# Issuing the input loads of batch 4 one phase earlier in a fused attention and feed-forward kernel

## Chip, cores and metric

The kernel runs on one core of a Trainium2 chip (trn2). The metric is the device time of one execution in microseconds (us). A profile's own span is some 1.7 to 1.9 us shorter than the device time of the same run.

## The reference

Eight batches of eight heads, 576 positions of 64 numbers. For each head, q is exponentiated and normalised along its 64 numbers, k along its 576 positions; the attention is linear. The result feeds a two-layer network with an exact GELU:

```python
q_s = softmax(q, axis=-1); k_s = softmax(k, axis=2)
kv  = einsum('bhsd,bhse->bhde', k_s, v)
x   = einsum('bhsd,bhde->bhse', q_s, kv)      # to (4608, 512), heads side by side
h   = x @ w_in                                 # 512 -> 2048
out = (0.5 * h * (1 + erf(h / sqrt(2)))) @ w_out   # 2048 -> 512, float32
```

## The kernel before

The tokens are worked in nine chunks: chunk c is 512 of the 576 positions of batch c, chunk 8 is what is left over of all batches. A chunk has a w_in phase (64 matmuls and 16 GELUs) and an output phase (four output tiles of 16 matmuls). In chunk c's phases the attention of later batches is prepared: loads, exponentials (ScalarE), normalisation (VectorE, GpSimd), a transpose by DMA, casts of v (VectorE), small matmuls. The parts that matter:

```python
def load(b):                       # three DMAs: 1024, 1152 and 1152 KB, two buffers each
    load_main(b, "q", q)
    load_pair(b, "k", k)
    load_pair(b, "v", v)

def cast_v_all(b):                 # four VectorE casts of v to bf16
    for hp in range(HP):
        cast_v(b, hp)

def y_out(c, ps, j):               # empties an output tile and stores it
    y_sb = moe_sb.tile([128, DM], FP32, tag="y_sb")     # four buffers
    nc.vector.tensor_copy(out=y_sb, in_=ps)
    ...
        nc.sync.dma_start(out=dst, in_=y_sb)

def y_phase(c, ins):
    for j in range(J - 1 if c == B else J):
        ps = psum_y.tile([128, DM], FP32, tag="y")      # two buffers
        for t in range(NDF):
            y_mm(c, ps, j, t)
            for f in ins.get((j, t), []):               # work hung in after matmul t of tile j
                f()
        y_out(c, ps, j)
...
y_phase(1, {
    (0, 15): [lambda: norm_q(2, 0, 2)],
    (1, 1): [lambda: norm_q(2, 1, 2, nc.vector)],
    (1, 12): [lambda: kv_step(2)],
    (1, 15): [lambda: xbar_step(2)],                    # the transpose by DMA
    (2, 2): [lambda: cast_v_all(3)],
    (3, 5): [lambda: x_all(2), lambda: kv_step(3)],
})

def front3():                      # hung into the w_in phase of chunk 2
    norm_q(3, 0, 2)
    norm_q(3, 1, 2, nc.vector)
    xbar_step(3)
    load(4)
...
    # chunk 2 onwards, nb = c + 2: hung into the output phase
    yi[(1, 0)] = [lambda nb=nb: norm_q(nb)]
    if nb < B:
        yi[(0, 8)] = [lambda nb=nb: cast_v_all(nb)]
    yi[(3, 0)] = [lambda nb=nb: xbar_step(nb)]
```

All loads, stores and transposes are issued by one queue (SyncE), in program order; only half of the last stores go by ScalarE's.

The softmax here doesn't subtract the row's maximum and nothing guards it: scores larger than these inputs give would overflow.

## Time and profile before

| | before |
|---|---|
| time, median of the first three runs | 283.32 us (283.0 to 283.43) |
| span of the profiled run | 281.7 us |
| TensorE busy | 272.7 us, 97% |
| VectorE, ScalarE, GpSimd busy | 36%, 56%, 12% |
| granted TensorE clock | 1.000 |

The page gives busy times, forty slices of the span, and a chain of waits that is followed back from the last instruction. TensorE is the bound from about 15 us on (busy 261.14 of the 263.20 us from there to 278.20). These lines of the chain show where TensorE's work ends (start, length, what); the span goes on to 281.66.

```profile
274.40 3.51 PE ps L326 x32
...
277.93 0.29 DVE y_sb L331
```

### The profile page before, as it was taken

To read this page: it belongs to the slowest core of one execution; us is meant where nothing else is said; L and a number is where in the kernel's file an instruction comes from. 1 tells how busy PE (TensorE), PEld (TensorE's weight loads), DVE (VectorE), ACT (ScalarE), POOL (GpSimd) and SP (SyncE) were. 2 spreads that over 40 slices of the span, in tenths; PEclk is the share of its full clock that TensorE was granted. 3 is DMA by queue.
4 is the path that set the end of the run, shared out by engine and by line. 5 is a ranking of instruction groups with operands and counts; after the bars stand their busy time and mean duration, and the time that the engine had idled before them with its cause. 6 is when DMAs were issued, how large, how long until landed. Compare 5 with 4: busy or idle time off the path is not lost.

```text
span 281.7 us, 4584 instructions
## 1 busy us (share of the span) xinstructions
PE 272.7 (97%) x1937; PEld 126.0 (45%) x1937; DVE 101.8 (36%) x149; ACT 156.8 (56%) x242; POOL 32.9 (12%) x25
## 2 busy tenths in 40 slices
PE   8789999999999899999999999999999999999994
PEld 3334454444444344444444444444444444444443
DVE  2766586309750570075006510562006200230021
ACT  5766754689467815693469436852683264036400
POOL 1530040002020050005000500050005000000000
PEclk9999999999999999999999999999999999999999
DMA  7999999952439329901990179226501500210033
GB/s 236 381 404 428 398 404 404 403 227 60 132 94 353 151 95 249 367 37 40 229 388 37 58 193 349 92 77 169 132 0 74 149 2 0 77 74 0 2 74 75
DMA packets 44851, 50.09 MB, mean 178 GB/s; under 512 B 20384, under 2 KB 29856, under 8 KB 44576
## 3 DMA queue, kind: packets, MB, share of 16 engines
q1 hardware_dynamic: 44544, 49.68, 51.7%
q8 instruction: 15, 0.25, 0.3%
q10 hardware_dynamic: 288, 0.13, 0.2%
q14 instruction: 4, 0.03, 0.0%
HBM read 36.70 MB, written 9.44 MB: 164 GB/s over the span
## 4 chain that ended last, share of the span: by engine, by line
PE 73%; DMA 18%; DVE 4%; ACT 2%; SPq 1%; issue 1%; ACTq 0%
PE ps L294 34%; PE ps L304 34%; DMA f<-in_v_dram 9%; DMA f<-in_q_dram 4%; DMA w<-in_moe_w_in_dram 3%; DMA touch<-in_moe_w_in_dram 2%; PE kv L165 2%; PE ps L250 1%; PE ps L326 1%; DVE v_aug L144 1%; DVE qsum L195 1%; ACT ek L137 1%; ACT e L132 1%; DVE e L197 1%; SPq L230 0%
## 5 line engine op out<-in xcount | busy, mean ns | idle before, releaser
L294 PE MATMUL ps<-xT,wi_bf 128*128 128x512 bf16 x576 | 126.1, 379 | 0.2 <-DVE wi_bf L378 0.2
L304 PE MATMUL ps<-wo_bf,g 128*128 128x512 bf16 x560 | 124.4, 379 | 1.3 <-DVE y_sb L311 1.3
L299 ACT ACTIVATE g<-ps 128x512 bf16<-128x512 f32 x144 | 85.6, 597 | 67.6 <-PE ps L294 67.6
L294 PEld LDWEIGHTS <-wi_bf 128*128 128x128 bf16 x576 | 56.1, 98 | 68.6 <-DVE wi_bf L378 0.7
L304 PEld LDWEIGHTS <-g 128*128 128x128 bf16 x560 | 53.9, 98 | 65.7 <-issue 1.9
L311 DVE COPY y_sb<-ps 128x512 f32<-128x512 f32 x35 | 23.9, 684 | 75.9 <-PE ps L304 75.6
L197 POOL TENSOR_TENSOR e<-e,recq 128x2048 bf16<-128x2048 bf16 (+1 forms) x9 | 25.7, 2857 | 178.0 <-DVE recq L196 145.9
L144 DVE CAST v_aug<-f 128x576 bf16<-128x576 f32 x26 | 17.9, 746 | 57.2 <-DMA f<-in_v_dram 57.2
L276 ACT CAST xT<-ps 128x512 bf16<-128x512 f32 x19 | 10.2, 588 | 31.0 <-PE ps L250 21.4
L195 DVE TENSOR_REDUCE qsum<-e 128x16 f32<-128x1024 bf16 (+1 forms) x13 | 21.0, 1614 | 15.1 <-ACT e L132 15.1
L132 ACT ACTIVATE e<-f 128x512 bf16<-128x512 f32 (+1 forms) x42 | 20.5, 556 | 1.8 <-DMA f<-in_q_dram 1.5
L137 ACT ACTIVATE ek<-f 128x2304 bf16<-128x2304 f32 (+1 forms) x10 | 17.2, 1730 | 3.1 <-DMA f<-in_k_dram 3.1
L274 DVE CAST xT<-ps 128x512 bf16<-128x512 f32 x15 | 9.7, 686 | 15.3 <-PE ps L250 12.4
L78 ACT ACT_TABLE_LOAD x9 | 11.5, 1283 | 2.8 <-issue 2.6
L404 PE MATMUL ps<-zeros 128*128 128x512 bf16 x29 | 8.8, 462 | 1.2 <-DVE scr L73 1.2
L132 ACT ACT_TABLE_LOAD x7 | 9.0, 1283 | 0.1
L165 PEld LDWEIGHTS <-ek 64*64 64x64 bf16 x576 | 6.6, 105 | 3.4 <-issue 1.2
L165 PE MATMUL kv<-v_aug,ek 64*64 64x65 bf16 x576 | 7.1, 193 | 0.7 <-POOL v_aug L144 0.4
L378 DVE CAST wi_bf<-w 128x512 bf16<-128x512 f32 (+1 forms) x8 | 7.1, 907 | 1.8 <-DMA w<-in_moe_w_in_dram 1.7
L397 DVE CAST wo_bf<-w 128x2048 bf16<-128x2048 f32 (+1 forms) x5 | 5.1, 1014 | 4.7 <-DMA w<-in_moe_w_out_dram 4.7
L197 DVE TENSOR_TENSOR e<-e,recq 128x1024 bf16<-128x1024 bf16 x4 | 6.4, 1606 | 0.1
L250 PE MATMUL ps<-qT,kvc 64*64 64x512 bf16 x60 | 5.0, 390 | 1.1 <-DVE kvc L176 1.0
(31 smaller groups left out, 41.1 us busy)
## 6 DMA issues: line engine op xcount, KB each, us to landing
out_dram<-y_sb SPq DMA_DIRECT2D x32, 256.0 KB, 2.3
f<-in_k_dram SPq DMA_DIRECT2D x6, 1152.0 KB, 9.5
f<-in_v_dram SPq DMA_DIRECT2D x6, 1152.0 KB, 11.4
f<-in_q_dram SPq DMA_DIRECT2D x6, 1024.0 KB, 7.1
w<-in_moe_w_in_dram SPq DMA_DIRECT2D x6, 512.0 KB, 7.9
f<-in_k_dram SPq DMA_DIRECT2D x4, 576.0 KB, 10.7
f<-in_v_dram SPq DMA_DIRECT2D x8, 288.0 KB, 8.4
f<-in_q_dram SPq DMA_DIRECT2D x4, 512.0 KB, 8.6
```

The source lines that it names most:

```text
L78: nc.scalar.activation(out=scr[:, 1:2], in_=scr[:, 0:1], func=func)
L132: nc.scalar.activation(out=dst[:, i], in_=src[:, u], func=AF.Exp)
L137: nc.scalar.activation(out=ek[b % 2][:, i:i + n], in_=st[b]["kf"][:, i:i + n].rearrange("p x (n d) -> p x n d", n=NS), func=AF.Exp,)
L144: eng.tensor_copy(out=v_aug[b % 2][:, hp, :, 0:D], in_=st[b]["vf"][:, hp, :].rearrange("p (n d) -> p n d", n=NS),)
L165: nc.tensor.matmul(ps[c, i, half, 0:D + 1], ek[b % 2][pr, hp, n, :], v_aug[b % 2][pr, hp, n, 0:D + 1], start=(n == 0), stop=(n == NS - 1),)
L195: nc.vector.reduce_sum(out=qsum, in_=eq[:, :, hs, :], axis=AX.X)
L197: eng.tensor_tensor(out=eq[:, :, hs, :], in0=eq[:, :, hs, :], in1=recq.unsqueeze(3).to_broadcast([128, J, w, D]), op=ALU.mult,)
L276: nc.scalar.copy(out=st[b]["xT"][:, hp, :], in_=ps)
L294: nc.tensor.matmul(ps, wi_bf[:, dm, t * 128:(t + 1) * 128], xT[:, dm, :], start=(dm == 0), stop=(dm == NDM - 1),)
L299: nc.scalar.activation(out=g[:, t, :], in_=ps, func=AF.Gelu)
L304: nc.tensor.matmul(ps, st[c]["g"][:, t, j * 128:(j + 1) * 128], wo_bf[:, t, :], start=(t == 0), stop=(t == NDF - 1),)
L311: nc.vector.tensor_copy(out=y_sb, in_=ps)
```

## The change

The loads of batch 4 waited in the issue queue behind the transpose of batch 3. The intent is to issue them one phase earlier, when their buffers have long been free.

```diff
-        (2, 2): [lambda: cast_v_all(3)],
+        (2, 2): [lambda: cast_v_all(3), lambda: load(4)],
...
         xbar_step(3)
-        load(4)
```

## The prediction

> **What bounds the kernel now.** I read the page first (busy shares, slices, chain), then the waits of TensorE, then a table by stage, then the timelines of VectorE and of the DMA-issuing queue around the one place where the chain leaves TensorE.
>
> ```profile
> PE 272.7 (97%) x1937; PEld 126.0 (45%) x1937; DVE 101.8 (36%) x149; ACT 156.8 (56%) x242; POOL 32.9 (12%) x25
> PEclk9999999999999999999999999999999999999999
> DMA  7999999952439329901990179226501500210033
> ```
>
> TensorE is busy 97% of the span at the full granted clock; all the others have room, and DMA is full only at the start and then in bursts, one per batch. TensorE sets the end. So the question is only whether the change moves an idle time of TensorE. In the whole stretch from 60 us to the end, the list of waits of TensorE has one row:
>
> ```profile
> PE ps L304 <- DVE y_sb L311: 1.3, 1, 1.3
> ```
>
> Line 304 is the output matmul, line 311 the copy that empties its PSUM tile. The wait happens once. The stage table puts it in a chunk. Its six rows are the hidden-layer (w_in) phase and the output phase of chunks 2, 3 and 4 in turn (start and end, length, then busy time by engine, clock, DMA share, GB/s):
>
> ```profile
> 76.26:90.07 13.81, 13.81 (x65) 6.27 (x64) 5.15 (x6) 8.79 (x15) 1.90 (x1) 1.00 0.60 185
> 90.07:106.60 16.53, 15.27 (x146) 7.13 (x144) 8.82 (x13) 8.64 (x11) 3.62 (x1) 1.00 0.39 149
> 106.60:120.41 13.81, 13.81 (x65) 6.27 (x64) 0.95 (x2) 8.96 (x15) 0.00 (x0) 1.00 0.95 304
> 120.41:135.54 15.13, 15.13 (x146) 7.16 (x145) 8.88 (x13) 8.64 (x11) 3.62 (x1) 1.00 0.19 61
> 135.54:149.35 13.81, 13.81 (x66) 6.26 (x65) 0.72 (x2) 8.96 (x15) 0.00 (x0) 1.00 0.90 296
> 149.35:164.47 15.12, 15.12 (x146) 7.12 (x145) 9.11 (x13) 8.64 (x11) 3.62 (x1) 1.00 0.19 60
> ```
>
> The w_in phases all take 13.81 us. The output phase of chunk 2 takes 16.53 where those of chunks 3 and 4, with the same work, take 15.13 and 15.12. The excess of 1.40 us is the only irregularity left. Its cause is in the chain of waits:
>
> ```profile
> 83.24 0.63 SPq L89
> ...
> 83.91 0.71 SPq L97
> ...
> 84.67 10.32 DMA f<-in_v_dram
> ...
> 95.01 2.73 DVE v_aug L144 x4
> 97.75 0.61 DVE y_sb L311
> ...
> 98.40 2.97 PE ps L304 x13
> ```
>
> The three issues at 83.24 to 85.18 us are q, k and v of batch 4, the very loads that the change moves. The v load lands at 94.99. The four casts of v (2.73 us) stand in VectorE's order ahead of the copy that empties the first output tile, so that copy starts at 97.66 and the third output tile, which reuses the same one of two PSUM tiles, starts at 98.40 where TensorE was ready at 97.14. The timeline of VectorE shows that nothing but the load held it:
>
> ```profile
> 79.96 1.75 DVE L197 TENSOR_TENSOR e<-e,recq 128x1024 bf16<-128x1024 bf16 x1
> 95.01 2.73 DVE L144 CAST v_aug<-f 128x576 bf16<-128x576 f32 x4 [13.30 <-DMA f<-in_v_dram]
> 97.66 0.68 DVE L311 COPY y_sb<-ps 128x512 f32<-128x512 f32 x1
> ```
>
> 13.30 us idle before the casts, ended by the v load.
>
> [...] batch 4 is issued 13.9 us before its phase boundary needs it (83.24 against 97.14) and takes 11.75 us to 94.99, and the casts and copy do not fit in the rest. [...] loads already follow the transpose of batch 3 by 0.05 us. [...] Here the rotation is two deep, so a copy that is late by more than one output tile (16 matmuls, about 3.5 us) stalls TensorE; the 1.26 us stall is that.
>
> **The change part by part.** Nothing is added or removed: the same three DMAs (1024, 1152 and 1152 KB), the same buffers, one core. Only the place in program order moves.
>
> Old place: behind the transpose of batch 3 in the issue queue, which waits for VectorE's normalisation to end at 81.71. Hence 83.24.
>
> New place: in the output phase of chunk 1, after its third output tile's third matmul. In the issue queue that is behind the transpose of batch 2 and the second store of chunk 1:
>
> ```profile
> 68.39 1.97 SPq L230 DMA_TRANSPOSE qT<-e  x1
> 70.46 7.05 SPq L314 DMA_DIRECT2D out_dram<-y_sb  x3
> 81.86 1.33 SPq L230 DMA_TRANSPOSE qT<-e  x1
> ```
>
> The second store takes 0.34 us to issue, so q is issued at about 70.46 + 0.34 + 0.05 = 70.85. Are the input buffers free? They are those of batch 2: its exponentials end on ScalarE at about 66.6, and its v was cast in chunk 1's w_in phase. Yes, so there is no new wait at the issue. The three issues take 0.63 + 0.71 + 0.51 and gaps, about 1.95 us, to 72.8, which is when the next store becomes ready (its copy ends at 72.77). So the issue queue loses nothing.
>
> Landing: with the old 11.75 us from the issue of q to the landing of v, v lands at about 70.85 + 11.75 = 82.6. VectorE is free from 81.71. The casts run at 82.6 to 85.3, inside the 13.30 us that VectorE sat idle. Then the first output tile of chunk 2 (ends about 90.07 + 3.5 = 93.6) is copied by 94.4, ahead of the 97.14 at which TensorE wants the PSUM tile: 2.7 us to spare, as in chunk 3, where the copy starts 3.66 us after the phase (124.07 against 120.41).
>
> The sum: chunk 2's output phase goes from 16.53 to about 15.13. That is the stall of 1.26 us plus 0.14 us that the table shows as longer busy time of the same matmuls (15.27 against 15.13), which I take for the restart after the stall. Everything after 98.40 is an unbroken TensorE chain to the last tile, so the saving passes whole to the end: 283.32 - 1.40 = 281.9 us. The next load, of batch 5, is issued after chunk 2's last store and so moves with TensorE; in chunk 3 its casts (120.15) already come before the first output copy (124.07).
>
> What earns nothing: q and k of batch 4 come earlier too, but the exponentials at 92.18 and 94.28 follow one another on ScalarE without a wait for them. Normalising batch 4 and its transpose start some 3 us earlier, and TensorE never waited for them.
>
> **The rivals.**
>
> (a) A collision with the transpose of batch 2. It is issued at 68.39, lands about 4.1 us later, at 72.5, and TensorE uses it at 72.89: only 0.4 us of slack, on the bounding engine. The loads now start right behind it. Against harm: they are behind it and behind a store in the same queue[...]; batch 3's transpose, with loads right behind it, landed in 3.7 us. If loads still shared the DMA engines with it, a landing 1 us late would cost 0.6 us, and the time would be about 282.5.
>
> (b) The wait moves to another place. The two stores of chunk 1 and the transpose of batch 3 now stand behind 3.3 MB of loads. The stores may land after 11 us; there are four output buffers, and the first to be reused is needed after 93. The transpose of batch 3 is issued at 81.86 with the loads nearly drained, and its product is used near 100. Even if the issue queue were held up by a full backlog (at start-up one k issue took 4.80 us), there are many us of room. This would leave the time at 281.9; only if it delayed the transpose by over 12 us would the gain go.
>
> (c) The load is hidden anyway and nothing changes, 283.3. The listed wait and the 16.53 against 15.13 speak against this.
>
> (d) DMA traffic slows the engines. The w_in phases at DMA shares of 0.60, 0.95 and 0.90 all take 13.81, so no.
>
> **Range and chances.** 281.9 us, a gain of 0.5%. The three runs of before lie within 0.43 us, and rival (a) can cost some tenths; a small shift in the loads at the start could move either side a little. Range 281.3 to 282.6. Since even removing all idle time left after 60 us is worth 0.5%, over 2% (5.7 us) in either direction needs a mechanism that I don't see: 1% faster, 98% same, 1% slower.
>
> **What would show each step.** Right: the list of TensorE's waits loses its row of 1.3 us from the output copy; batch 4's loads are issued near 71 and its casts begin near 82.6; the output phase of chunk 2 takes about 15.1 us; every later event is 1.3 to 1.4 us earlier. Wrong: a TensorE gap before the attention matmuls at 72.9 or a transpose of batch 2 landing in over 4.5 us (rival a); casts beginning later than 94 (the loads held by something I missed); or an output phase of chunk 1 that has grown.

The 11 us of rival (b) is the longest landing of a store in the profile before (11.0; median 2.3).

## The result, and the profile after

| | before | after |
|---|---|---|
| median, 6 runs each | 283.26 us (282.64 to 283.58) | 282.6 us (281.98 to 283.68) |
| ratio | | 0.998, 95% interval 0.9959 to 1.0001 |
| span of the profiled run | 281.66 us | 280.79 us |

A ratio is the mean time of one kernel's fast runs over that of the other's fast runs of the same rounds, so not quite the ratio of the medians. 0.998 is 0.57 us. The forecast was 1.40. By this first timing even the 0.57 is not clear of zero: the interval reaches 1.0001.

Yet the stage that the prediction was about became as short as it said. The stage table of the changed kernel, its rows of the output phases of chunks 2 and 3:

```profile
89.93:105.05 15.12, 15.12 (x145) 7.11 (x144) 6.41 (x9) 8.64 (x11) 3.62 (x1) 1.00 0.19 61
...
118.86:133.98 15.12, 15.12 (x146) 7.14 (x145) 9.02 (x13) 8.64 (x11) 3.62 (x1) 1.00 0.19 61
```

The output phase of chunk 2 takes 15.12 us, like that of chunk 3; it had taken 16.53. The list of TensorE's waits has no row left from 44 us to the end. The timelines of the issue queue and of VectorE show the steps: q is issued at 70.89, the casts begin at 85.28 (before: 95.01), and the output copy waits for TensorE at 93.59, not the other way about.

```profile
70.89 0.42 SPq L89 DMA_DIRECT2D f<-in_q_dram  x1
71.41 0.66 SPq L97 DMA_DIRECT2D f<-in_k_dram  x1
72.11 0.51 SPq L97 DMA_DIRECT2D f<-in_v_dram  x1
```

```profile
85.28 2.73 DVE L144 CAST v_aug<-f 128x576 bf16<-128x576 f32 x4 [3.71 <-DMA f<-in_v_dram]
93.59 0.69 DVE L311 COPY y_sb<-ps 128x512 f32<-128x512 f32 x1 [5.58 <-PE ps L304]
```

The end of the chain, after:

```profile
272.86 3.51 PE ps L326 x32
...
276.38 0.29 DVE y_sb L331
```

TensorE and the last copy finish 1.55 us earlier than before (276.38 against 277.93), but the span only 0.87 us earlier. What follows the last copy has grown. The DMA view of that last stretch shows it, before (from 278.3 us on) and then after (from 276.7 us on): queues with packets, MB and share, and the last two stores with KB and us from issue to landing.

```profile
q1 hardware_dynamic: 160, 0.13, 16.7%
q10 hardware_dynamic: 160, 0.13, 12.8%
...
out_dram<-y_sb SPq DMA_DIRECT2D x1, 32.0 KB, 2.0
out_dram<-y_sb ACTq DMA_DIRECT2D x1, 32.0 KB, 2.1
```

```profile
q1 hardware_dynamic: 160, 0.13, 13.9%
q10 hardware_dynamic: 160, 0.13, 11.2%
q14 instruction: 1, 0.01, 0.5%
...
out_dram<-y_sb SPq DMA_DIRECT2D x1, 32.0 KB, 3.0
out_dram<-y_sb ACTq DMA_DIRECT2D x1, 32.0 KB, 3.1
```

After, one instruction fetch (8 KB, on queue 14) runs while the last stores are under way, and they land 3.0 and 3.1 us after their issue, not 2.0 and 2.1. Before, that fetch comes when all is over. The only difference in VectorE's instruction list is one wait for a semaphore, in front of the first output copy of chunk 2 (193 instructions before, 194 after); SyncE too has one wait more (171 instructions before, 172 after). I read the wait as follows: before, the cast's wait for the v load covered what the copy needed, and now that it waits on another semaphore, the copy needs one of its own. The semaphore records agree: before, the v load and the cast's wait used semaphore 109; after, both use 105, and the added wait is for 109. No run tested it apart from that.

### The profile page after: what moved, and what is told of

The parts are those of the page before. It is cut to its first block, busy times and chain, and to the rows that moved or that the text cites. A ratio compares the mean times of both kernels' runs of the same rounds, so it can differ in the third digit from the quotient of the medians.

```text
span 280.8 us, 4586 instructions
## 1 busy us (share of the span) xinstructions
PE 273.0 (97%) x1937; PEld 125.9 (45%) x1937; DVE 102.1 (36%) x149; ACT 156.8 (56%) x242; POOL 32.9 (12%) x25
## 4 chain that ended last, share of the span: by engine, by line
PE 89%; DMA 6%; ACT 2%; SPq 1%; DVE 1%; issue 1%; ACTq 0%
PE ps L294 43%; PE ps L304 41%; DMA w<-in_moe_w_in_dram 3%; DMA f<-in_v_dram 3%; PE kv L165 2%; PE ps L250 1%; PE ps L326 1%; ACT ek L137 1%; ACT e L132 1%; ACT L132 0%; DVE wi_bf L378 0%; SPq L97 0%; SPq L89 0%; PE ps L211 0%; PE ps L255 0%
```

## The experiments

**How they are read.** The start varies from run to run by about as much as the effect (46.13 and 44.97 us in two profiles of the same kernel), so each profile is cut into parts whose scatter is known. The table is made from the instruction and DMA records of the traces. "Opening" is the time until the w_in phase of chunk 1 starts; "body" from there to the end of the last copy; "chunk 2" from the start of its w_in phase to the start of chunk 3's; "tail" from the end of the last copy to the end of the span; "fetch" the start of the nearest 8 KB instruction fetch on queue 14, counted from the end of the last copy. The ratio is to the kernel before in the same rounds, its interval beside it.

```text
run             opening  chunk 2  body    tail  fetch  VectorE instr.  median   ratio (95%)
before           46.13   30.34   232.10  3.44   +3.77      193        283.26
b_again          44.97   30.29   232.05  3.45   +3.77      193        283.37   0.9996 (0.9975-1.0017)
after            46.00   28.93   230.68  4.12   +1.63      194        282.60   0.9980 (0.9959-1.0001)
a_again          46.09   28.93   230.72  4.08   +1.59      194        282.34   0.9966 (0.9948-0.9985)
c_cast_later     45.58   28.93   230.68  4.07   +1.59      194        282.30   0.9967 (0.9949-0.9986)
d_extra_old      46.23   35.16   237.01  4.01   +1.59      194        289.44   1.0220 (1.0191-1.0250)
e_extra_new      45.49   28.93   230.68  4.02   +1.60      194        282.23   0.9972 (0.9950-0.9994)
f_v_first        45.64   28.93   230.75  4.10   +1.62      194        282.32   0.9977 (0.9956-0.9998)
pad1_before      47.67   31.22   232.98  4.14   +1.66      194        286.69   1.0140 (1.0111-1.0169)
pad8_after       47.95   28.93   230.71  3.15   -9.53      202        282.96   0.9995 (0.9972-1.0019)
idle1_before     46.24   30.26   232.02  4.23   +1.59      194        284.27   1.0037 (1.0016-1.0059)
idle8_after      46.52   28.93   230.68  3.12   -9.51      202        281.81   0.9946 (0.9929-0.9962)
shift8_after     47.12   28.93   230.68  4.11   +1.63      194        283.85   1.0020 (1.0003-1.0036)
shift64_after    47.85   28.93   230.68  4.12   +1.64      194        284.37   1.0038 (1.0021-1.0056)
minus1_after     45.91   28.93   230.71  3.44   +3.75      193        281.89   0.9957 (0.9945-0.9970)
idle3_after      45.92   28.93   230.69  3.12   -0.04      197        281.17   0.9925 (0.9913-0.9938)
shift256_after   45.99   28.93   230.68  4.10   +1.61      194        282.52   0.9977 (0.9964-0.9990)
```

Opening, body and tail of a row are one profile; median and ratio are of all its runs. All effects here are below 2%, except that of d_extra_old, whose interval holds the 2%.

**a_again: the changed kernel once more.** No edit.

> The changed kernel itself, once more. Theory 1 (the saving of 1.4 us passes whole to the end of TensorE's work, and the shortfall in the first timing is scatter of the start and of the last stores): mean of the rounds 1.2 to 1.6 us below the kernel before; output phase of chunk 2 at 15.1 us; last TensorE work ends 1.2 to 1.8 us earlier relative to the start of chunk 2. Theory 2 (something in the change gives back about 0.8 us each time, such as later last stores): mean 0.4 to 0.8 us below, and the last stores again land 3.0 us or more after issue.

Measured: 0.96 us below before (ratio 0.9966). Body 230.72 and tail 4.08, as in the first profile. Body less by 1.4, tail more by 0.65: 0.7 to 0.75 net, which lies inside both timings' intervals. The 0.96 lies between the ranges of the two theories, so the time alone does not decide. The profiles do: the body is shorter by the full 1.4, as theory 1 said, and something is given back in the tail each time, as theory 2 said. That the shortfall is mere scatter falls.

**b_again: the kernel before against itself.** No edit.

> The kernel before against itself: the scatter of the measure. Both theories: ratio 1.000, within 0.15%. Theory 1 expects that the time from the last copy to the end of the span varies by some tenths of a us here too (3.8 us in the first profile of before, 4.4 in that of after), Theory 2 that it stays at 3.8.

Ratio 0.9996. Body and tail repeat to 0.05 us (232.05, 3.45), while the opening came 1.16 us earlier. (The 3.8 and 4.4 of the expectation count from the start of the last copy.) This tells scatter from effect: the opening scatters, the tail repeats with the program.

**c_cast_later: the stall removed without moving a load.**

```diff
-                yi[(0, 8)] = [lambda nb=nb: cast_v_all(nb)]
+                yi[(1, 8) if c == 2 else (0, 8)] = [lambda nb=nb: cast_v_all(nb)]
```

> The loads stay in their old place, but the four casts of v of batch 4 are put after the first output copy of chunk 2 instead of ahead of it. The stall goes without any load moving. Theory 1: no wait of TensorE for the output copy, output phase of chunk 2 at 15.1 us, the same time as the changed kernel (1.2 to 1.6 us below before). Theory 2, that early loads cost something: 1.4 us below before, and better than the changed kernel by about 0.8 us.

```profile
93.17 0.69 DVE L311 COPY y_sb<-ps 128x512 f32<-128x512 f32 x1 [12.01 <-PE ps L304]
...
96.51 2.67 DVE L144 CAST v_aug<-f 128x576 bf16<-128x576 f32 x4
```

VectorE's timeline has the copy ahead of the casts, and the stall is gone although v lands about as late as before (94.31 us, before 94.99). Body 230.68 and tail 4.07 are those of the changed kernel, and so is the time: 0.93 us below before, less than either theory expected. Two things follow. The stall was the order of cast and copy together with the late v. And the long tail does not come from moving the loads: here none moved, but VectorE has its extra wait here too. SyncE has not (171 instructions, as before; 172 after), so its extra wait is not the cause either.

**d_extra_old: the stall made longer.**

```diff
         xbar_step(3)
+        load_wo(1)      # 1 MB, read again and not used
         load(4)
```

> The kernel before with one more load of 1 MB (read again and not used) ahead of the loads of batch 4 in their old place. It makes v land later by about 2.6 us (1 MB at the 400 GB/s that the trace shows). Theory 1: the stall grows from 1.26 to about 3.9 us and the time by 2.6 us (2.3 to 2.9): one to one. If a part of such a stall were absorbed further on, the time would grow by under 2 us.

Expected 2.6, measured 6.2 us. The wait, then the stage table with its row of chunk 2's output phase and two parts of it:

```profile
PE ps L304 <- DVE y_sb L311: 4.5, 1, 4.5
```

```profile
90.26:111.61 21.35, 16.80 (x145) 7.48 (x144) 8.82 (x13) 8.64 (x11) 3.62 (x1) 0.92 0.46 168
101.88:105.00 3.12, 3.12 (x8) 1.17 (x8) 3.02 (x3) 0.00 (x0) 0.39 (x1) 0.50 0.22 84
105.00:106.30 1.30, 1.30 (x7) 0.39 (x4) 0.01 (x1) 0.00 (x0) 1.30 (x1) 1.00 0.30 115
```

The stall grew by 3.28 us (4.54 against 1.26), since v landed that much later. On top, the granted clock was 0.50 in the 3.12 us after the stall (0.92 over the whole phase, 1.00 from 105.00 on): the matmuls that start in those 3.12 us come every 0.43 us, not every 0.22. By my estimate from these intervals (seven of them, 0.21 us longer each) that costs about 1.5 us, and 3.28 + 1.5 is the 4.82 by which chunk 2 grew (35.16 against 30.34). With the longer tail (0.57) that makes 5.4, and the profiled run took 5.6 us more than that of before (289.04 against 283.44). The rest of the 6.2, which is of all runs, was not traced. After 4.54 us without a matmul the clock was 0.50; after the 1.26 us of before it was 1.00 (98.40 to 101.50 us). That the idle time lowered the clock is my reading; no run tested it apart, nor from what length of idle time on.

**e_extra_new: the same extra load in the new place.**

```diff
-        (2, 2): [lambda: cast_v_all(3), lambda: load(4)],
+        (2, 2): [lambda: cast_v_all(3), lambda: load_wo(1), lambda: load(4)],
```

> The changed kernel with the same extra 1 MB load as in the earlier experiment, ahead of the loads of batch 4 in their new place. In the old place it cost 6.2 us. In the new place the casts would end at 85.3 + 2.7 + 2.6 = 90.6 us and the first output copy waits for nothing before 93.6: no stall, start of chunk 1 to last copy at 230.7 us, time as the changed kernel within 0.3%. If the early loads were near the limit, the stage of chunk 2 would grow.

```profile
86.40 2.73 DVE L144 CAST v_aug<-f 128x576 bf16<-128x576 f32 x4 [5.32 <-DMA f<-in_v_dram]
93.08 0.69 DVE L311 COPY y_sb<-ps 128x512 f32<-128x512 f32 x1 [3.95 <-PE ps L304]
```

The casts end at 89.1, four microseconds before the copy is wanted. Body 230.68: what cost 6.2 us in the old place costs nothing here. The early place has room to spare.

**f_v_first: old place, other order.**

```diff
-        load(4)
+        load_pair(4, "v", v)
+        load_main(4, "q", q)
+        load_pair(4, "k", k)
```

> The kernel before with its loads of batch 4 in the old place, but in the order v, q, k instead of q, k, v. v then lands near 88 instead of 95 us, and the stall should go: chunk 2 at 28.9 us as in the changed kernel, start of chunk 1 to last copy 230.7 us. k lands last, at about 95, and its exponential starts 0.7 us later on ScalarE, which delays nothing on TensorE. Tail by the tail theory 4.0 to 4.1 if VectorE gets the extra wait instruction, else 3.44; time 0.7 to 1.4 us below before.

```profile
88.87 2.73 DVE L144 CAST v_aug<-f 128x576 bf16<-128x576 f32 x4 [7.58 <-DMA f<-in_v_dram]
```

v starts its casts at 88.87 and the copy at 93.30 waits 1.70 us for TensorE. The body is 230.75. A third way to the same body, with the same tail of 4.10. The time is 0.65 us below before (0.06 to 1.25), just short of the expected 0.7 to 1.4.

**pad1_before and pad8_after: the tail theory, first try.** One and eight tiny memsets on VectorE in its idle stretch.

```diff
     scr = singles.tile([128, 2], FP32)
+    pad = singles.tile([128, 2], FP32)
...
         xbar_step(3)
+        for _ in range(1):          # 8 in pad8_after
+            nc.vector.memset(pad, 0.0)
```

> The kernel before with one more tiny instruction (a memset of 128x2 that nobody reads) on VectorE, put where VectorE is idle for 13 us. New theory (the tail): in all profiles with 194 VectorE instructions an 8 KB instruction fetch runs 1.6 us after the last copy, among the last stores, and the time from the end of the last copy to the end of the span is 4.0 to 4.1 us; with 193 (before, twice) the fetch comes at 3.8 us, after the end, and it is 3.44 us. So this one instruction alone must make that tail 4.0 to 4.1 us with the fetch at 1.6, leave the rest (start of chunk 1 to last copy) at 232.1 us, and cost 0.6 us in time (0.2%). Rival (the longer tail comes from the earlier end[...], not from the instruction count): the tail stays at 3.4.

> The changed kernel with eight such tiny instructions on VectorE in its idle stretch. By the tail theory the instruction fetch moves to an earlier output phase, away from the last stores: tail 3.5 us or less, start of chunk 1 to last copy at 230.7 us as in the changed kernel, so the full 1.4 us below before (1.2 to 2.0) and 0.6 us or more below the changed kernel. Rival: tail 4.1 as in the changed kernel, no gain over it.

The tails did as the theory said: 4.14 with one instruction more than before, 3.15 with eight more than after. The times did not: plus 1.4% and minus 0.05%. The opening took 47.7 and 48.0 us, and in pad1_before the stall also grew, from 1.3 to 2.1 us; opening, body and tail of its profile are 3.1 us above before's, of the 4.0 us that the 1.4% stand for. The loads were slower: the stage table of pad1_before, from 10 to 40 us, against the same stretch of a_again (last number, GB/s):

```profile
10.00:40.00 30.00, 27.73 (x208) 12.53 (x209) 18.83 (x24) 20.27 (x32) 6.36 (x8) 1.00 1.05 389
```

```profile
10.00:40.00 30.00, 27.98 (x208) 12.57 (x207) 19.53 (x26) 21.81 (x34) 6.36 (x8) 1.00 1.05 408
```

The edit had done two things at once: added instructions, and put a tile of 8 bytes per partition ahead of all later tiles. The next six runs take them apart.

**idle1_before and idle8_after: instructions alone.** The memsets go into a buffer of a pool that exists.

```diff
         xbar_step(3)
+        idle = small.tile([128, J, H // 2], FP32, tag="qsum")
+        for _ in range(1):          # 8 in idle8_after
+            nc.vector.memset(idle[:, 0, 0:2], 0.0)
```

> The clean form of the earlier run with one extra VectorE instruction: the kernel before with one memset of 128x2 in VectorE's idle stretch, but into a buffer that exists already, so that no address moves. Tail theory: instruction fetch 1.6 us after the last copy, tail 4.0 to 4.1 us against 3.44, start of chunk 1 to last copy unchanged at 232.1; start of chunk 1 at 45.0 to 46.1 us as in the other runs without a moved address (it was 47.7 with the added tile). Time 0.6 us (0.2%) above before. If the opening is late here too, it is the instruction that makes it so and not the address.

> The changed kernel with eight such instructions into the existing buffer. Tail theory: fetch 9 us or more before the last copy, tail 3.15 us (4.1 in the changed kernel), start of chunk 1 to last copy 230.7; start of chunk 1 at 45.0 to 46.1. Time about 0.9 us below the changed kernel and 1.7 us (0.6%) below before: the version that should beat both.

The last stretch of idle1_before in the DMA view:

```profile
q14 instruction: 1, 0.01, 0.8%
...
out_dram<-y_sb SPq DMA_DIRECT2D x1, 32.0 KB, 3.1
out_dram<-y_sb ACTq DMA_DIRECT2D x1, 32.0 KB, 3.2
```

One VectorE instruction that does nothing, put 195 us before the end, turned the tail from 3.44 into 4.23 us with the body unchanged (232.02), and the time of before rose by 1.05 us (0.45 to 1.67), of which the tail explains 0.79. Eight in the changed kernel moved the fetch to 9.5 us before the last copy; the last stores landed in 2.0 and 2.1 us, the tail became 3.12 and the time 1.53 us below before. The opening of idle8_after was the latest of the runs without a moved address, 46.52, at 402 GB/s; I count that as scatter.

**minus1_after: one VectorE instruction less.**

```diff
-        nc.vector.memset(scr, 0.0)
+        nc.gpsimd.memset(scr, 0.0)
```

> The changed kernel with one VectorE instruction less: the memset of the table-load scratch at the start is done by GpSimd. VectorE is back at 193 instructions. Tail theory: the fetch comes after the end again and the tail is 3.44 us as in the kernel before; start of chunk 1 to last copy 230.7; time 0.65 us below the changed kernel and 1.3 us (0.45%) below before. Rival (the tail belongs to the moved loads and not to the count): tail 4.1.

Back at 193 VectorE instructions the fetch comes at +3.75, the tail is 3.44 to the hundredth, the body 230.71. The time is 1.22 us below before (0.9957): nearly the 1.40 of the prediction. The moved loads do not make the tail long.

**idle3_after: how far the fetch must move.** As idle8_after, with three.

> The changed kernel with three idle VectorE instructions into an existing buffer. The last VectorE instructions before the end are the two last copies (0.9 us apart), the copy before them 2.6 us earlier, each with a wait or two. Three more instructions should set the fetch off one or two copies earlier, between 2 us before and 1 us after the last copy. If it falls before the last stores' data (from 0.5 us after the last copy) the tail is 3.1 to 3.5, if among them 4.1. Start of chunk 1 to last copy 230.7.

The fetch starts 0.04 us before the end of the last copy, and that is enough: the last stores land in 2.0 and 2.1 us and the tail is 3.12. The time, 281.17 us, is the best: 0.9925 of before. That is 2.1 us (1.8 to 2.5), of which body and tail explain 1.4 + 0.3; the rest is not explained and I do not claim it. This is the version that beats both kernels.

**shift8_after, shift64_after, shift256_after: the address alone.** An unused tile of 8, 64 or 256 bytes per partition; no instruction is added.

```diff
     scr = singles.tile([128, 2], FP32)
+    unused = singles.tile([128, 2], FP32)      # [128, 16], [128, 64]
```

> The changed kernel with a tile of 8 bytes per partition that nothing uses, which moves the addresses of the later tiles by 8 bytes; no instruction is added. If the moved address slows the loads (GB/s of the opening near 376 instead of 404), the start of chunk 1 comes at 47.5 to 48.0 us and the time is 1.5 us or more above the changed kernel; tail 4.1. If the address is without effect, 45.0 to 46.1 and no difference.

> The same with an unused tile of 64 bytes per partition. If what matters is where in a 64-byte line the tiles begin, the loads run as in the changed kernel: start of chunk 1 at 45.0 to 46.1 us, no difference in time. If any move of the addresses is harmful, 47.5 or later.

> The changed kernel with an unused tile of 256 bytes per partition. [...] opening at 404 GB/s, start of chunk 1 at 45.0 to 46.1 us, time as the changed kernel. If every move is harmful: 376 GB/s, 47 us or later, 1.2 us or more above.

The stretch from 10 to 40 us of shift8_after, then of shift256_after:

```profile
10.00:40.00 30.00, 27.89 (x207) 12.57 (x208) 18.92 (x25) 20.93 (x33) 6.36 (x8) 1.00 1.05 390
```

```profile
10.00:40.00 30.00, 28.37 (x217) 13.20 (x219) 19.47 (x26) 21.75 (x34) 6.35 (x8) 1.00 1.05 408
```

8 and 64 bytes slow the loads from 408 to 390 GB/s and bring chunk 1 in 1 to 2 us late; 256 bytes do nothing (45.99 us, ratio as the changed kernel's). In this stretch the four profiles with tiles moved by 8 or 64 bytes show 389 or 390 GB/s, the thirteen others 402 to 408. The 8 bytes did less than expected: 47.12 us instead of 47.5 or more, and a time 1.1 to 1.5 us above the changed kernel's two timings instead of 1.5 or more. What the expectation of shift64_after supposed, a 64-byte line, is ruled out; in that of shift256_after the first figures, those of a move without effect, held. In shift64_after (390 GB/s as well) the granted clock was also down to 0.94 in this stretch, so part of its 47.85 us may be that; but two other runs of it at a clock of 1.000 took 284.31 and 285.09 us, so its longer time does not hang on the clock. These loads write to the tiles that moved; why a move by 8 or 64 bytes slows them and one by 256 does not is not shown, and the addresses themselves were not looked at.

## Why the prediction was wrong

What bounds the kernel, and the stall: right. One wait of 1.26 us, from late v through casts and copy; the change, c_cast_later and f_v_first take it away each in its own way and get the same body.

The issue of q at 70.85 (measured 70.89), no new wait at the buffers, casts inside VectorE's idle time, chunk 2's output phase at 15.13 (15.12): right. The landing of v was put at 82.6 and came at 85.26: 14.37 us after the issue of q, not the old 11.75. The DMA engines moved 4.60 MB in that stretch against 3.92 MB in the old one, as parts of two transposes and of stores went through it too; that this is the reason was not tested. It cost nothing.

The 1.40 us, as a saving up to the last copy: right. The body fell from 232.07 (mean of 232.10 and 232.05) to 230.70 (of 230.68 and 230.72), by 1.37.

Two steps failed. The first: "Nothing is added or removed". One wait instruction was added on VectorE, and one on SyncE. The second: "the saving passes whole to the end". It passed whole to the last matmul and copy, but the time after them is not a constant. It went from 3.44 to 4.10 us because the extra VectorE instruction brought an 8 KB instruction fetch forward into the last stores (from 3.77 to 1.63 us after the last copy). 1.37 - 0.66 is 0.71 us, against 0.57 and 0.96 in the two timings. Adding an idle instruction to before (tail 4.23) and taking one from after (tail 3.44) show this cause from both sides; that the fetch is VectorE's is shown by the count of VectorE's instructions alone moving it (+3.77 us at 193, +1.59 at 194 in idle1_before, -0.04 at 197, -9.51 at 202).

The semaphore and DMA records show how the fetch delays the stores. A landing is counted in sixteen parts. In after, fifteen parts of the last two stores land by 2.30 us after the last copy, about as before (all by 2.18); one part of each lands at 2.98 and 3.16. The fetch ends at 1.94, and from then to 2.35 the last packets of the stores follow; before, they were through at 1.76. So, by these times, a small part of the stores waits behind the fetch, and the program waits for that part.

Rivals: (a) the collision with the transpose cost nothing: it landed in 4.1 us, and TensorE's start of the attention matmuls moved by no more than the 0.13 us by which all was earlier. (b) named the right kind of thing, a delay that moves to another place, but sought it in the stores of chunk 1 and not at the end. Where it looked, the loads were not nearly drained: the transpose of batch 3 took 4.77 us to issue, not 1.33, and landed in 6.8 us, not 3.7, without making TensorE wait. (c) and (d) were rightly set aside. The range was also too tight on its own ground: it rested on three runs of before within 0.43 us, and eleven runs of before on one chip later spread over 1.5 us (282.63 to 284.11).

The traces also show where the tails of 3.44 and 3.12 differ, though the stores land alike. In before, b_again and minus1_after, the three profiles in which the fetch has not come by the end, VectorE's last DRAIN (a step of the program's end) comes 0.40 us after SyncE's; in the fourteen others it comes 0.03 to 0.04 us after. GpSimd's closing step follows it, at 3.25 us after the last copy in before and at 2.93 in idle3_after. So VectorE itself is late at the very end when its fetch has not come yet; why is not shown.

What stays open: why the late part of a store lands 0.8 us after its last packet (2.35 to 3.16) and not 0.4 as before (1.76 to 2.18); why VectorE is late at the end; and what makes the opening scatter.

## What to carry to other kernels

When TensorE never waits, look past it. Here time was lost and won in the last stores and in the first loads, by edits that did not touch them: one idle VectorE instruction made the last stores land after 3.1 and 3.2 us instead of 2.0 and 2.1 and the tail 4.23 us instead of 3.44 (idle1_before), and an unused tile of 8 bytes per partition made the opening 47.12 us instead of 46.00 (shift8_after: loads at 390 GB/s instead of 408). A ratio within half a per cent should be read by parts (opening, body, tail): in the two profiles of before the body repeats to 0.05 us, the tail to 0.01, the opening only to 1.16. And an experiment that adds a tile may have moved the tiles after it: take a buffer that exists (openings of 46.24 and 46.52 us in idle1_before and idle8_after), or round it to 256 bytes, which did nothing here (45.99).
